# A layer pair of segmented memory attention: the second scores without their wait for the first half's logarithm, and GpSimd's copies of old rows ordered behind the fold

## The chip, the cores and the metric

The kernel runs on one core of a Trainium2 chip. The metric is the device time of one launch in microseconds (us). The core has five engines that run side by side and wait for each other through semaphores: TensorE (PE in the profile; its weight loads are PEld), VectorE (DVE), ScalarE (ACT), GpSimd (POOL) and SyncE (SP, which here only issues DMAs). Each engine works through its instructions in order.

## The reference

Two layers of the same form, each an attention with a recurrent memory (A) and then a gated MLP (B). The attention runs through 64 segments of 32 rows. Eight rows of memory stand in front of each segment, and the first eight rows of the output are the memory of the next segment, so segment after segment must wait for the one before.

```
for s in range(n_seg):                      # 2048 / 32 = 64
    h = concat([mem, xs])                   # 8 + 32 rows of 512
    q, k, v = h @ Wq, h @ Wk, h @ Wv        # 32 heads of 128
    p = softmax(where(mask, q k^T * scale, -1e9))
    o = (p @ v) @ Wo
    mem = o[:8]; outs.append(o[8:])
x = x + A(layernorm(x)); x = x + B(layernorm(x))   # twice
```

## The kernel before

**Tiling.** A block is 128 rows, four segments; j4 is a segment's place in its block and tb the block. Queries and keys of a segment's 24 new rows and 8 memory rows are made in the segment itself, from hT. The last eight rows of every segment are "old rows": their queries, keys and values are known without the memory and are made a block ahead by `b_units`, in pieces that `fill()` puts between the segment's own products. Their source is hB, a GpSimd copy (L637, called by `ln_turn` in a segment with j4 = 0) of the normalized rows that a DMA transpose brought into hT. Their results land by DMA transposes in the tiles KTB and QTB (in the profile: "front" or "old").

**A set of copies.** `prep_segment(s)` moves a segment's old rows from there into QQ (L877, one copy) and KX (L881, one copy for each half r of the heads), on GpSimd. QQ and KX have two buffers (NKQ = 2), so segments s and s + 2 share one. `prep_segment(s + 1)` stands at the end of segment s in the code.

**A segment in order** (`segment`, L905 and on). The products of queries and keys (L714) go through ScalarE (L924) and VectorE (transposes, L927) into QQ and KA. `scores(0)` (L950 for the new keys, L954 for the old keys in KX) writes the first bank of psS; `exps(0)` (L959) and `close(0)` (L962, the exponentials times the mask, giving E) follow. `sums_zero` (L976) adds up the weights of the first half into psS[:, 0, 224:384], called pN. `inverse` makes their reciprocal in RN, as a logarithm (L1017) and an exponential (L1018) on ScalarE. `scores(1)` writes the second bank of psS. Because both halves are in one tile, the scheduler would let it wait for every reader of the tile; `other_bank` declares some of these readers no dependency. Then come `exps(1)`, `close(1)` (the second L962), the division of the first half's weights by their sums (`divide_main` L992, `divide_own` L997), the sums of the second half (`sums_one`, L987), the products with the values (L1004, L1007) and the output product (L790, L797). The fold (L887, L889 and `build_hA` with L896 and L897) adds the parts of that product up, writes the memory of the next segment to memT in two halves of 64 columns (k = 0, 1) and transposes them into hT.

**Order.** PE, DVE and ACT are in the order in which the code is written. The instructions of GpSimd and SyncE are put in order by the scheduler, from its own estimate of when each is ready; what stands ahead in that order is waited for. GpSimd also issues DMAs: loads and stores of the rows that the residual is added to (L222, L224, L229, L240), and near the end of a layer the loads of the MLP's weights (L173, L174). In the last four segments of a layer it adds rows itself (L228), behind a small copy that orders it (`seen`, L1179).

Of the kernel before, what the change touches and what calls it, by code (L numbers as in the profile page):

```python
# [9 lines left out]
ACT = mybir.ActivationFunctionType  # L10
# [4 lines left out]
P = 128  # L15
# [654 lines left out]
def a_block(tc, c, rows, front, MV_in, RS_in, MV_out, RS_out, ahead, wo, S, first):  # L670
    nc = tc.nc
# [5 lines left out]
    with ExitStack() as ctx:  # L677
# [39 lines left out]
        def other_bank(mms, *reads):  # L717

            for m in mms:
                for r in reads:  # L720
                    tc.declare_no_dep(m.ins, r.ins, reason="another bank of the tile")

        memT = [pers.tile([P, P], BF16, name=f"memT{i}") for i in range(2)]
        NKQ = 2
        KAr = [pers.tile([P, 2, 8, 32, 2], BF16, name=f"KA{i}") for i in range(2)]
        QQr = [pers.tile([P, 2, 8, 40, 2], BF16, name=f"QQ{i}") for i in range(NKQ)]
        KXr = [pers.tile([P, 4, 2, 32], BF16, name=f"KX{i}") for i in range(NKQ)]
# [145 lines left out]
        def prep_segment(s, eng=nc.gpsimd):  # L873
            tb, j4 = s // 4, s % 4
            bs = blk_state[tb]
            QQ = QQr[s % NKQ]
            eng.tensor_copy(QQ[:].rearrange("p r n q two -> p (r n) two q")[:, :, :, 32:40],  # L877
                            bs["QTB"].rearrange("p r (n two) k -> p (r n) two k", two=2)[:, :, :, 8 * j4:8 * j4 + 8])
            KX = KXr[s % NKQ]
            for r in range(2):  # L880
                eng.tensor_copy(KX[:, :, r].rearrange("p g (k i) -> p i g k", i=4),  # L881
                                      bs["KTB"][:, r].rearrange("p (i g) k -> p i g k", i=4)[:, :, :, 8 * j4:8 * j4 + 8])
            seg_state[s] = dict(QQ=QQ, KX=KX, VX=bs["VX"])

# [20 lines left out]
        def segment(s, fill, spare1, spare2, spare3, tail, loads):  # L905
            tb, j4 = s // 4, s % 4
            st = seg_state.pop(s)
            QQ, KX, VX = st["QQ"], st["KX"], st["VX"]
            KA = KAr[s % 2]
# [9 lines left out]
            def qk_mm(j, ps, kts=range(KT)):  # L919
                return mm_chunk(ps, lambda kt, cg: hA_cur[:, kt, :], lambda kt, cg: qk_rhs(w, j, kt, cg), kts)  # L920
# [5 lines left out]
            def qk_T(j, r):  # L926
                nc.vector.transpose(out=(QQ[:, j % 2, :, 0:32] if j < 2 else KA[:, j % 2]).bitcast(F32).rearrange("p n q one -> p n (q one)"), in_=r[:].bitcast(F32))  # L927

            def v_mm(r, ps, kts=range(KT)):
                return mm_chunk(ps, lambda kt, cg: hA_cur[:, kt, :], lambda kt, cg: cols_rhs(w, 4 + r, kt, cg), kts)  # L930

            def ends(q):

                return q.rearrange("p h (b e) -> p h b e", e=8)[:, :, 0:5:4, :]

            def own(q):

                return q.rearrange("p (i b e) -> p i b e", i=4, b=2)
# [4 lines left out]
            def scores(r):  # L943

                pS = psS[:, r, :]
                mms = []
                for i in range(4):
                    for g in range(4):
                        n = 4 * i + g
                        mms.append(nc.tensor.matmul(pS[32 * g:32 * g + 32, 40 * i:40 * i + 40], lhsT=KA[:, r, n // 2, :, n % 2], rhs=QQ[:, r, n // 2, :, n % 2],  # L950
                                                    start=(i == 0), stop=True, tile_position=(0, 32 * g), skip_group_check=True))
                for g in range(4):
                    q = QQ[:, r].rearrange("p (i g) q two -> p i g two q", i=4)[:, :, g // 2, g % 2, :]
                    mms.append(nc.tensor.matmul(own(pS[32 * g:32 * g + 32, 160:224]), lhsT=KX[:, g, r, :], rhs=ends(q),  # L954
                                                start=False, stop=True, tile_position=(0, 32 * g), skip_group_check=True))
                return mms

            def exps(r):
                return nc.scalar.activation(out=S[:, r], in_=psS[:, r, 0:224], func=ACT.Exp, scale=scale)  # L959
# [53 lines left out]
            def hview(t, r, lo, hi):  # L1013
                return t.rearrange("p (r g n) q -> p r g n q", r=2, g=2)[:, r, :, :, lo:hi]

            def inverse(out, src):
                nc.scalar.activation(out=out, in_=src, func=ACT.Ln)  # L1017
                return lambda: nc.scalar.activation(out=out, in_=out, func=ACT.Exp, scale=-1.0)  # L1018

            def rview(R, q):  # L1020
                return R[:].rearrange("p g (n q) -> p g n q", q=q)
# [16 lines left out]
            qk_mm(3, psK[:, 0, :], (0, 1, 2))  # L1038
            psS = att.tile([P, 2, 512], F32, name="psS")
            scores(0)  # L1040
            exp0 = exps(0)
            qk_mm(3, psK[:, 0, :], (3,))
            r3, read = qk_rows(psK[:, 0, :])
            if begin:
# [3 lines left out]
            pN = psS[:, 0, 224:384]  # L1048
            sums_zero(pN)
            RN = segp.tile([P, 160], F32, name="RN", bufs=1)  # L1050
            invert = inverse(RN[:], pN)
            invert()
            qk_T(3, r3)
            nc.vector.tensor_copy(VA[:, 0].rearrange("p i e -> p (i e)"), psK[:, 1, :])
            if j4 == 0 and tb + 1 < NB and not begin:
# [2 lines left out]
                fill()  # L1058
            psW = accB.tile([P, 512], F32, name="psV")
            v_mm(1, psW, (0, 1))  # L1060
            other_bank(scores(1), exp0)
            v_mm(1, psW, (2, 3))
            exps(1)
            nc.scalar.copy(VA[:, 1].rearrange("p i e -> p (i e)"), psW[:])
# [14 lines left out]
            if not begin:  # L1079
                fill()  # L1080
            pT = psT[:, :, 0:320].rearrange("p g (n q) -> p g n q", q=40)
            inverse(rview(Rm, 8), pT[:, :, :, 0:8])()
            nc.vector.tensor_tensor(out=uM[1], in0=oview(1, 0, 8), in1=rview(Rm, 8), op=ALU.mult)
            Rt = segp.tile([P, 2, 256], F32, name="Rt", tag="Rt", bufs=1)
            invert = inverse(rview(Rt, 32), pT[:, :, :, 8:40])
            nc.scalar.copy(uT_[0], oview(0, 8, 32))
            nc.scalar.copy(oL[0], oview(0, 32, 40))
# [31 lines left out]
            if s + 1 < NSEG:  # L1119
                prep_segment(s + 1)  # L1120
# [14 lines left out]
        start = nc.vector if first else nc.gpsimd  # L1135
        rows.begin(start)
        prep_segment(0, start)
        due, ys = [], []
        seen = pers.tile([P, 1], BF16, name="seen")
# [16 lines left out]
        for s in range(NSEG):  # L1156
# [78 lines left out]
            def loads():  # L1235
                if due and s < NSEG - 1 and (not ys or tb == NB - 1):
# [7 lines left out]
                    else:  # L1244
                        y_load(y, wo.VX[0][:].rearrange("p j r e -> p (j r e)").bitcast(F32))

            segment(s, lambda n=1: [next(more, None) for _ in range(n)], spare1, spare2, spare3, tail, loads)
        assert due == [NB - 5] and ys == [[NB - 6, True]]
        for k in range(3):
# [57 lines left out]
```

## Time and profile before

| | us |
|---|---|
| median of 3 runs (lowest, highest) | 1660.8 (1657.8, 1661.63) |
| the profiled execution | 1662.02 |
| its span, first to last instruction | 1660.3 |
| granted TensorE clock | 0.997 |
| one segment: first scores to the next segment's first scores, median | 10.3 |
| GpSimd, L881 KX<-old, 128 copies | 63.8, mean 0.522 each |
| GpSimd, L877 QQ<-old, 64 copies | 40.3, mean 0.630 each |
| VectorE, L962 E<-S,maskN, 256 products | 119.0, mean 0.465 each |
| GpSimd, L637 hB<-hT, 30 copies: idle before them, until the DMA hT<-ln_xn | 159.2 |

In lines of the timeline the columns are the start in us from the beginning of the span, the length in us, the engine, the source line, the operation, output<-inputs, the sizes (partitions x elements) and the count; a bracket gives the engine's idle time before and what ended it. In the groups of a page the columns are busy time and mean length of one in ns, then the idle time before. A matmul's end is modelled, and GpSimd's spans are rough.

### The profile page before, as it was taken

What the parts mean: (1) busy time and instruction counts of PE and PEld (TensorE: products, weight loads), DVE (VectorE), ACT (ScalarE), POOL (GpSimd) and SP (SyncE); (2) the same over time, 40 slices, a digit from 0 to 9 for tenths busy, and PEclk for the clock granted to TensorE, in tenths of its full rate; (3) what the DMA queues carried; (4) which work ended last, traced back from release to release, by engine and by line L of the source; (5) the groups of instructions that cost most, each with busy time, mean ns of one, the idle gap of its engine ahead of it and who ended that gap; (6) DMA issues with size and microseconds to landing.
All of it is one profiled execution on the core that took longest, in us unless ns stands there. A gap on an engine that the chain in (4) does not pass through costs nothing.

```text
span 1660.3 us, 88316 instructions
## 1 busy us (share of the span) xinstructions
PE 1603.2 (97%) x39646; PEld 981.6 (59%) x39646; DVE 1117.0 (67%) x3308; ACT 1038.0 (63%) x2409; POOL 306.2 (18%) x604
## 2 busy tenths in 40 slices
PE   5799999999999999999999999999999999999999
PEld 2455566666666666566655556666666666665565
DVE  3566667767777777785466666666677667767722
ACT  2577777777777777661047777777777777766400
POOL 5111111112211222320011111111122112214100
PEclk9999999999999999999999999999999999999999
DMA  9211111112321333277961111112233223335697
GB/s 364 80 42 42 42 41 42 42 42 74 80 55 42 73 84 83 90 171 153 201 179 45 46 47 43 47 42 47 60 91 78 51 55 96 87 68 157 145 202 159
DMA packets 263603, 148.85 MB, mean 90 GB/s; under 512 B 197560, under 2 KB 239648, under 8 KB 263224
## 3 DMA queue, kind: packets, MB, share of 16 engines
q1 hardware_dynamic: 249992, 99.38, 26.9%
q0 software_dynamic: 13232, 43.82, 8.2%
q8 instruction: 310, 5.08, 1.3%
q14 instruction: 69, 0.57, 0.1%
HBM read 59.68 MB, written 37.19 MB: 58 GB/s over the span
## 4 chain that ended last, share of the span: by engine, by line
PE 88%; DVE 5%; DMA 3%; ACT 1%; issue 1%; POOL 0%; SPq 0%; DVEq 0%; POOLq 0%; ACTq 0%
PE psK L714 13%; PE psQ L714 12%; PE psb L714 10%; PE pg L397 9%; PE px L790 7%; PE psO L797 7%; PE psm L714 7%; PE psV L714 6%; PE pwB L809 3%; PE psS L950 3%; PE pz L296 3%; PE psT L987 3%; PE py L440 2%; PE psO L1004 2%; DMA Wk_sb<-in_A_Wk_dram 1%; PE psO L1007 1%
## 5 line engine op out<-in xcount | busy, mean ns | idle before, releaser
L714 PEld LDWEIGHTS <-hT 128*32 128x32 bf16 x12288 | 323.7, 96 | 249.6 <-DVE hT L897 44.9
L924 ACT CAST rows<-psQ 128x512 bf16<-128x512 f32 x256 | 147.9, 588 | 115.1 <-PE psQ L714 114.9
L927 DVE STREAM_TRANSPOSE QQ<-rows 128x256 f32<-128x256 f32 x256 | 113.8, 444 | 120.9 <-ACT rows L924 120.4
L714 PE MATMUL psV<-Wv_sb,hT 128*32 128x512 bf16 x2048 | 157.7, 378 | 0.0
L397 PE MATMUL pg<-z,wspT 128*128 128x344 bf16 x1024 | 154.5, 309 | 0.2 <-DMA wspT<-in_B_w_sp_dram 0.2
L714 PE MATMUL psK<-Wk_sb,hT 128*32 128x512 bf16 x2048 | 152.4, 379 | 0.0
L714 PE MATMUL psQ<-Wq_sb,hT 128*32 128x512 bf16 x2048 | 136.8, 381 | 12.7 <-DVE hT L897 7.5
L927 DVE STREAM_TRANSPOSE KA<-rows 128x256 f32<-128x256 f32 x256 | 113.9, 445 | 51.0 <-ACT rows L924 39.3
L797 PE MATMUL psO<-Wo_high,uT 128*32 128x128 bf16 x8192 | 137.6, 219 | 0.5 <-issue 0.5
L714 PE MATMUL psm<-Wq_sb,hT 128*32 128x512 bf16 x2048 | 136.0, 381 | 1.3
L790 PE MATMUL px<-Wo,uT 128*32 128x256 bf16 x3840 | 134.5, 274 | 1.8 <-DVE uT L1077 1.8
L714 PE MATMUL psQ<-Wk_sb,hT 128*32 128x512 bf16 x2048 | 136.2, 381 | 0.0
L714 PE MATMUL psK<-Wv_sb,hT 128*32 128x512 bf16 x2048 | 134.2, 378 | 0.0
L962 DVE TENSOR_TENSOR E<-S,maskN 128x448 bf16<-128x448 bf16 x256 | 119.0, 465 | 19.1 <-ACT S L959 2.3
L397 PEld LDWEIGHTS <-wspT 128*128 128x128 bf16 x1024 | 100.1, 98 | 53.7 <-DMA wspT<-in_B_w_sp_dram 0.5
L797 PEld LDWEIGHTS <-uT 128*32 128x32 bf16 x8192 | 127.3, 97 | 2.4 <-issue 0.6
L714 PEld LDWEIGHTS <-hB 128*32 128x32 bf16 x2976 | 85.6, 97 | 72.2 <-issue 19.2
L950 PEld LDWEIGHTS <-KA 128*32 128x32 bf16 x4096 | 67.6, 94 | 83.9 <-DVE KA L927 51.0
L959 ACT ACTIVATE S<-psS 128x224 bf16<-128x224 f32 x256 | 91.8, 359 | 38.8 <-PE psS L954 30.2
L881 POOL COPY KX<-old 128x128 bf16<-128x128 bf16 x128 | 63.8, 522 | 267.6 <-PE psS L954 122.9
L790 PEld LDWEIGHTS <-uT 128*32 128x32 bf16 x4096 | 97.8, 96 | 23.4 <-DVE uT L1077 20.3
L881 POOL COPY KX<-front 128x128 bf16<-128x128 bf16 x126 | 62.2, 521 | 248.2 <-PE psS L954 101.5
(205 smaller groups left out, 3019.1 us busy)
## 6 DMA issues: line engine op xcount, KB each, us to landing
o_d<-o_sb SPq DMA_DIRECT2D x126, 64.0 KB
vb_d<-front SPq DMA_DIRECT2D x30, 256.0 KB
VX<-vb_d SPq DMA_DIRECT2D x120, 64.0 KB
ln_x<-xd SPq DMA_DIRECT2D x26, 256.0 KB
y_o<-o_d POOLq DMA_DIRECT2D x22, 256.0 KB, 3.5
xd<-y_o POOLq DMA_DIRECT2D x22, 256.0 KB, 3.1
Wq_sb<-in_A_Wq_dram POOLq DMA_DIRECT2D x8, 512.0 KB, 8.4
Wk_sb<-in_A_Wk_dram POOLq DMA_DIRECT2D x8, 512.0 KB, 10.0
```

Source lines behind the costliest of these rows:

```text
L296: nc.tensor.matmul(pz[:, c0:c1], lhsT=xnT[:, kt, :], rhs=w_in_sb[:, kt, c0:c1], start=(kt == 0), stop=(kt == KT - 1))
L397: nc.tensor.matmul(pg[t][:, k, 0:344], lhsT=wsp[t][:, st, :], rhs=z(st, 344 * k, 344 * k + 344), start=(st == 0), stop=(st == NT - 1))
L714: return [nc.tensor.matmul(ps[32 * cg:32 * cg + 32, :], lhsT=lhs(kt, cg), rhs=rhs(kt, cg), start=(kt == 0), stop=(kt == KT - 1), tile_posi ...
L790: nc.tensor.matmul(px[at:at + 32, 0:256], lhsT=lhs[:, h, :], rhs=wo_rhs(h, slice(k + 2, None, -2) if h % 2 else slice(k, None, 2)), start= ...
L797: nc.tensor.matmul(pw[32 * cg:32 * cg + 32, :], lhsT=lhs[:, h, :], rhs=wo_rhs(h, cg), start=False, stop=(h == H - 1), tile_position=(0, 32 ...
L809: nc.tensor.matmul(pwB[32 * t:32 * t + 32, :], lhsT=src[:, h, :], rhs=wo.head(h).rearrange("p (kt g el) -> p g kt el", kt=4, g=4), start=( ...
L881: eng.tensor_copy(KX[:, :, r].rearrange("p g (k i) -> p i g k", i=4), bs["KTB"][:, r].rearrange("p (i g) k -> p i g k", i=4)[:, :, :, 8 * ...
L924: return r, nc.scalar.copy(r[:].rearrange("p (n el two) -> p n el two", n=8, two=2), ps.rearrange("p (n two el) -> p n el two", n=8, two=2))
L927: nc.vector.transpose(out=(QQ[:, j % 2, :, 0:32] if j < 2 else KA[:, j % 2]).bitcast(F32).rearrange("p n q one -> p n (q one)"), in_=r[:]. ...
L950: mms.append(nc.tensor.matmul(pS[32 * g:32 * g + 32, 40 * i:40 * i + 40], lhsT=KA[:, r, n // 2, :, n % 2], rhs=QQ[:, r, n // 2, :, n % 2], ...
L959: return nc.scalar.activation(out=S[:, r], in_=psS[:, r, 0:224], func=ACT.Exp, scale=scale)
L962: nc.vector.tensor_tensor(out=E[:, r], in0=S[:, r].unsqueeze(1).to_broadcast([P, 2, 224]), in1=maskN[:], op=ALU.mult)
```

## The change

There are two parts. In `segment`, the logarithm on pN is put in the list of readers that `other_bank` declares to be no dependency of `scores(1)`: it reads the first bank, the scores write the second. In `prep_segment`, for every segment but the first, a one-column copy of memT[s % 2] goes into a place of QQ ahead of the QQ copy, and one into a place of KX ahead of each KX copy. The copies that follow overwrite these places, so no value changes. The column is the last of memT, which the second half of the fold writes.

```diff
@@ prep_segment
             QQ = QQr[s % NKQ]
+            if s > 0:
+                eng.tensor_copy(QQ[:, 0, 0, 32:33, 0], memT[s % 2][:, P - 1:P])
             eng.tensor_copy(QQ[:].rearrange("p r n q two -> p (r n) two q")[:, :, :, 32:40],
                             bs["QTB"].rearrange("p r (n two) k -> p (r n) two k", two=2)[:, :, :, 8 * j4:8 * j4 + 8])
             KX = KXr[s % NKQ]
             for r in range(2):
+                if s > 0:
+                    eng.tensor_copy(KX[:, 0, r, 0:1], memT[s % 2][:, P - 1:P])
                 eng.tensor_copy(KX[:, :, r].rearrange("p g (k i) -> p i g k", i=4),
                                       bs["KTB"][:, r].rearrange("p (i g) k -> p i g k", i=4)[:, :, :, 8 * j4:8 * j4 + 8])
@@ segment
-            def inverse(out, src):
-                nc.scalar.activation(out=out, in_=src, func=ACT.Ln)
+            def inverse(out, src, log=None):
+                (log if log is not None else []).append(nc.scalar.activation(out=out, in_=src, func=ACT.Ln))
                 return lambda: nc.scalar.activation(out=out, in_=out, func=ACT.Exp, scale=-1.0)
...
             scores(0)
-            exp0 = exps(0)
+            reads = [exps(0)]
...
-            invert = inverse(RN[:], pN)
-            invert()
+            inverse(RN[:], pN, reads)()
...
-            other_bank(scores(1), exp0)
+            other_bank(scores(1), *reads)
```

## The prediction

> **What bounds the kernel now.** I read the page first: the shares of the engines and the chain that ended last.
>
> ```profile
> PE 1603.2 (97%) x39646; PEld 981.6 (59%) x39646; DVE 1117.0 (67%) x3308; ACT 1038.0 (63%) x2409; POOL 306.2 (18%) x604
> PE 88%; DVE 5%; DMA 3%; ACT 1%; issue 1%; POOL 0%; SPq 0%; DVEq 0%; POOLq 0%; ACTq 0%
> ```
>
> TensorE ends the chain nearly everywhere, so a saving counts only where TensorE stands still. A mean over the span can't show that, so next I read the timeline of one segment (number 45 of 128, start and length in us).
>
> ```profile
> 515.55 0.45 DVE L927 STREAM_TRANSPOSE KA<-rows 128x256 f32<-128x256 f32 x1
> 515.62 0.62 PE L714 MATMUL psV<-Wv_sb,hT 128*32 128x512 bf16 x8
> 515.91 0.30 ACT L1017 ACTIVATE RN<-psS 128x160 f32<-128x160 f32 x1 [0.39 <-PE psS L976]
> 516.05 0.38 PEld L950 LDWEIGHTS <-KA 128*32 128x32 bf16 x16 [0.31 <-DVE KA L927]
> 516.24 0.34 ACT L1018 ACTIVATE RN<-RN 128x160 f32<-128x160 f32 x1
> 516.26 0.28 PE L950 MATMUL psS<-QQ,KA 128*32 128x40 bf16 x16
> 516.65 0.36 ACT L959 ACTIVATE S<-psS 128x224 bf16<-128x224 f32 x1
> 516.74 0.70 POOL L877 COPY QQ<-old 128x256 bf16<-128x256 bf16 x1 [1.49 <-PE psS L954]
> 516.83 0.83 PE L714 MATMUL psb<-Wq_sb,hB 128*32 128x512 bf16 x12
> 517.04 0.59 DVE L962 TENSOR_TENSOR E<-S,maskN 128x448 bf16<-128x448 bf16 x1
> 517.68 0.37 PE L987 MATMUL psT<-E,ones 64*128 64x320 bf16 x4
> ```
>
> Two stops are here. The weights of the second scores (KA, done at 516.00) load at 516.05, but the first product starts at 516.26, 0.05 us after the logarithm of L1017 ends at 516.21; in all 128 segments that distance is 0.05. And L962 takes 0.59 us while GpSimd copies QQ; the sums at L987 start 0.05 after it ends. Next the same stretch of segment 46, where GpSimd copies no QQ at that moment:
>
> ```profile
> 527.45 0.83 PE L714 MATMUL psb<-Wq_sb,hB 128*32 128x512 bf16 x12
> 527.66 0.39 DVE L962 TENSOR_TENSOR E<-S,maskN 128x448 bf16<-128x448 bf16 x1
> 528.21 0.36 PE L987 MATMUL psT<-E,ones 64*128 64x320 bf16 x4
> ```
>
> L962 takes 0.39 and ends at 528.05; L987 starts 0.16 later, behind the products of the fill. Counted over the trace, the second L962 of a segment takes over 0.5 us in 85 segments of 128. From the first scores to the first product of L790 these take 4.38 us in the median (j4 = 0: 4.45), the other 43 take 4.26.
>
> **Part one, the logarithm.** One wait goes in each segment. What ends last then? KA allows a load at 516.05; the eight value products before it start at 515.62 and leave two rounds of 0.21 us (the spacing of four 512-column products in the trace), so TensorE is free at 516.05 too. The scores can start at 516.06 to 516.16 (at once, or after a load of 0.10), that is 0.10 to 0.20 earlier; I take 0.14, between the ends because a load is partly covered by the wait today. Nothing else has to move: the exponential of L1018 stays, and L959 behind it on ScalarE is ready by then. In the 43 free segments TensorE leads into L987, so 43 x 0.14 = 6.0 us (4.3 to 8.6). In the other 85 alone this part would give nothing much, since L962 decides there.
>
> **Part two, the copies leave the closing products.** A set of old-row copies (one QQ, two KX) runs a segment and more ahead today, in the middle of a segment. Now three one-column copies of memT go in front of each set, 378 in all, and the set overwrites that column. In the built program's order the first waits for the second L896 of the fold (k = 1); QQ and KX follow. GpSimd starts 0.16 to 0.18 us after what releases it (L881 behind L954); there VectorE runs L897, L902, L1115 and L927. In today's trace these take the same under a GpSimd copy as without: 246 and 245 ns, 252 and 251, 541 and 540, 445 and 445. So the place is free for VectorE and the second L962 falls to 0.39 everywhere.
>
> With both parts, L987 starts at the later of two: TensorE's products (a free segment's 3.31 us after the first scores, less 0.14) or L962. L962 starts when S is there (0.03 behind L959) and L992 has gone on; between L992 and L962 lie 0.37 at least and 0.42 mostly in the trace, so it gains 0 to 0.06, ends at 3.09 to 3.15 and allows L987 at 3.14 to 3.20. TensorE's 3.17 lies between. Against today's 3.40 in contended segments that is 0.20 to 0.26, and from L987 on the free segments are faster by a further 0.03 (L1007 waits for L997 today). I take 0.255 (0.23 to 0.29): 85 x 0.255 = 21.7 us (19.5 to 24.7). Gain of both parts: 27.7 us (23.8 to 33.3).
>
> At L992 a rule differs from the row. The Trainium skill, GPSIMD Engine Reference, section 8 (Key points), says that GpSimd contends with VectorE instructions that have two SBUF inputs. L992 has two, yet its median is 492 ns with a copy beside it and without; were it stretched like the others and fell to its shortest, 450 ns, the gain would be up to 85 x 0.04 = 3.6 us larger. I keep the row.
>
> **Part three, what the copies now wait for, and what waits behind them.** GpSimd works in order. A set costs, from the first small copy: 0.20 for a 128x1 copy (L1179), 0.30 from the end of a GpSimd instruction to one that waits for it (the store behind L228), then QQ, then KX 0.38 later, and 0.47 for KX:
>
> ```profile
> 37.55 0.47 POOL L877 COPY QQ<-front 128x256 bf16<-128x256 bf16 x1
> 37.94 0.72 POOL L881 COPY KX<-front 128x128 bf16<-128x128 bf16 x2
> ```
>
> That is 0.20 + 0.30 + 0.38 + 0.47 = 1.35 us to the first KX, plus 0.1 to 0.2 to start and some 0.15 until TensorE sees it (from 0.05, what VectorE needs, to 0.30): 1.65 us. Normally there is time: from the fold to the first scores lie 3.2 to 3.3 us. But in the built order the hB copy (L637), which waits for a DMA transpose of the next block's rows, stands ahead of the set in the first segment of a block; today it stands behind sets that are long done. In segment 116 a weight load (L173) stands between as well:
>
> ```profile
> 1395.17 0.29 POOL L637 COPY hB<-hT 128x128 bf16<-128x128 bf16 x1 [4.71 <-DMA hT<-ln_xn]
> 1395.69 0.54 POOL L173 DMA_DIRECT2D front<-in_B_w_in_dram  x1 [0.23 <-issue]
> ```
>
> The first scores there start at 1396.04 today, so their KX would come 1.7 us late. Taking the margin from hB's end (or that load's) to the first KX product for all 28 such segments, 13 have less than 1.65 us; the shortfalls sum to 8.7 us. With 1.30 us for a set they sum to 4.3, with 2.20 to 17.9.
>
> In the last segment of each layer the set stands behind the row additions, and behind two weight loads:
>
> ```profile
> 1513.23 0.54 POOL L173 DMA_DIRECT2D front<-in_B_w_in_dram  x1
> 1513.76 0.54 POOL L174 DMA_DIRECT2D front<-in_B_w_in_dram  x1
> ```
>
> Its KX products are due at 1512.82: 1514.30 + 1.65 - 1512.82 = 3.1 us late; in the first layer 702.04 + 1.65 - 702.64 = 1.05. With the 0.2 that segment 62 gains, 4.6 us (3.9 to 5.7). The DMAs queued behind a set (y loads and stores of 0.54 us issue) are late by the set, about 1.2 us; the trace shows GpSimd idle before most of them. SP's transposes into the old rows wait for reads that end a segment earlier: nothing. The small copies themselves lie on GpSimd, busy 18%.
>
> **Sum.** -27.7 + 8.7 + 4.6 = -14.4 us on the profiled execution's 1662.0 (span 1660.3, 1.7 around it). The median of the runs is 1660.8, 1.2 below that execution; from it, about 1647. The ends: -33.3 + 4.3 + 3.9 gives 1636, -23.8 + 17.9 + 5.7 gives 1661.
>
> **The rivals.**
>
> The copies are never late: the transposes land early enough or a set takes under 1 us. For it: the margins reach 3.0 us. Against: eleven of them are below 1.25, and the last segments' loads are late whatever. With 1.0 us for a set the shortfalls sum to 1.7 and the ends to 3.3: -27.7 + 5, 1638. Chance 0.14.
>
> The stretch of L962 moves instead of going: L962 stays near 0.59 for another reason, or the sums are held by L992 and ScalarE. Then part one gives its 128 x 0.05 (the least that L959 can use), 6 us, against 13 of part three: 1668, slower. Against: the second L962 under a QQ copy take 0.59 us in the median, the others 0.39. Chance 0.05.
>
> Late copies outweigh all. Place: the first scores of a block's first segment and of the last segment, L950 and L954. If each GpSimd copy waits out the one before (0.30 each) and its wake-up is slow, a set takes 3.0 us; then the 28 margins fall short by 36.9 us and the ends by 7.3, so +16.5 us: 1677, slower. It decides from a set of 2.4 us (22.2 + 5.9 us, the gain). For it: extra waits for DMAs stand ahead of QQ and KX in just these segments. Against: two KX copies in a row start 0.27 apart in the trace, so copies overlap. Chance 0.10.
>
> Gain and late copies cancel, a set of 2.2 us with the low gain (-23.8 + 17.9 + 5.7): 1661. Chance 0.08.
>
> **How the numbers follow.** The forecast has 0.63. A measurement can tell about 0.2%, 3.3 us. Faster: 0.63 and 0.14, with 0.02 of the cancelling case, 0.79; within 0.2%: its other 0.06; slower: 0.10 and 0.05. The range, 1635 to 1660, holds the forecast, the never-late case and half of the cancelling one, and leaves out the two slower ones.
>
> **What would show it.** In the changed profile: L950 of the second scores starts within 0.16 us of KA, not 0.05 after L1017; the second L962 is 0.39 in nearly all segments; QQ and KX copies of 0.47 lie within 2 us of the fold; first scores to L790 about 4.12 us. TensorE idles before L950 or L954, released by GpSimd, in some 13 first segments and in the last of each layer, 13 us together. It is wrong if those waits are in most segments, if the copies lie under L962 still, or if L987 stays where it was because L962 starts later.

## The result, and the profile after

The changed kernel takes 1644.9 us in the median of four runs (1641.5 to 1648.0), beside 1660.6 us for the kernel before on the same chip (1657.8 to 1661.6): ratio 0.9908, 95% interval 0.9879 to 0.9937, 0.9% faster. A second set of runs gave 0.9903 (0.9888 to 0.9919). The profiled execution took 1647.84 us with a span of 1646.1, 14.2 us below that of before, at a granted clock of 0.993 (before: 0.997).

The page of the changed kernel, the busy times and the chain that ended last:

```profile
PE 1586.1 (96%) x39646; PEld 967.9 (59%) x39646; DVE 1090.9 (66%) x3308; ACT 1022.8 (62%) x2409; POOL 303.7 (18%) x982
PE 89%; DVE 3%; issue 3%; DMA 2%; ACT 1%; POOL 1%; POOLq 0%; DVEq 0%; ACTq 0%
```

GpSimd has 378 more instructions (982 for 604), yet is busy 2.5 us less: its copies no longer lie beside VectorE's closing products, and are shorter for it (QQ: 0.48 us in the median, 0.70 before). DVE's share of the chain fell from 5% to 3%, and GpSimd, which had none, has 1%. Next the timeline of segment 45, the stretch shown of before (lines 927, 950, 1017, 992, 962 and 987 are now 931, 954, 1021, 996, 966 and 991):

```profile
509.25 0.45 DVE L931 STREAM_TRANSPOSE KA<-rows 128x256 f32<-128x256 f32 x1
509.60 0.31 ACT L1021 ACTIVATE RN<-psS 128x160 f32<-128x160 f32 x1 [0.39 <-PE psS L980]
509.75 0.28 PE L954 MATMUL psS<-QQ,KA 128*32 128x40 bf16 x16
510.31 0.49 DVE L996 TENSOR_TENSOR E<-E,RN 128x320 bf16<-128x320 bf16 x1
510.72 0.38 DVE L966 TENSOR_TENSOR E<-S,maskN 128x448 bf16<-128x448 bf16 x1
511.16 0.37 PE L991 MATMUL psT<-E,ones 64*128 64x320 bf16 x4
```

The second scores start at 509.75, 0.05 us after KA is done (509.70) and while the logarithm still runs (to 509.91). In the median of all segments they start 0.158 before the logarithm's end, where before they started 0.051 after it. The second L966 takes 0.38 instead of 0.59; products over 0.5 us fell from 85 segments to 2. In these two (62 and 127) no copy lies beside L966 but a row addition of GpSimd's (L228), here in segment 62:

```profile
687.03 0.49 DVE L996 TENSOR_TENSOR E<-E,RN 128x320 bf16<-128x320 bf16 x1
687.05 1.48 POOL L228 TENSOR_TENSOR rowsB<-rowsB,y_x 128x512 f32<-128x512 f32 x1 [2.61 <-DMA rowsB<-o_d]
687.44 1.35 DVE L966 TENSOR_TENSOR E<-S,maskN 128x448 bf16<-128x448 bf16 x1
```

The sums at L991 start 3.20 us after the first scores (before: 3.40 in contended segments), and L790 starts 4.15 after them instead of 4.38. The copies now stand right behind the fold, here ahead of segment 25:

```profile
299.39 0.18 DVE L900 TENSOR_TENSOR memT<-psO,t 128x64 bf16<-128x64 f32 x1
...
299.70 0.19 POOL L878 COPY QQ<-memT 128x1 bf16<-128x1 bf16 x1 [6.91 <-DVE memT L900]
299.83 0.30 POOL L884 COPY KX<-memT 128x1 bf16<-128x1 bf16 x2
300.07 0.47 POOL L879 COPY QQ<-front 128x256 bf16<-128x256 bf16 x1
300.46 0.76 POOL L885 COPY KX<-front 128x128 bf16<-128x128 bf16 x2
```

The small copy starts 0.13 us after the fold's second half ends, and QQ takes its undisturbed 0.47. The first KX copy ends 1.24 us after the start of the first small copy (median of all sets), the second 1.54.

Where the 14.2 us come from: summed over the 128 segments, the time from the first scores to L790 fell from 570.8 to 547.9 us, late KX copies included. From L790 to the next first scores (without the step from layer to layer) it rose from 757.6 to 767.0 us; 3.7 of that is the last segment of the second layer, 1.2 segments 52 and 116 (GpSimd's queue, below), and about 2 are two stops of 1 us in which TensorE waits for nothing that the profile shows. The other 2.5 us lie scattered, in both directions, and are not explained. The two stretches together give 13.5 of the 14.2 us.

### The profile page after: what moved, and what is told of

The parts are those of the page before. It is cut to its first block, busy times and chain, and to the rows that moved or that the text cites. A ratio compares the mean times of both kernels' runs of the same rounds, so it can differ in the third digit from the quotient of the medians.

```text
span 1646.1 us, 88740 instructions
## 1 busy us (share of the span) xinstructions
PE 1586.1 (96%) x39646; PEld 967.9 (59%) x39646; DVE 1090.9 (66%) x3308; ACT 1022.8 (62%) x2409; POOL 303.7 (18%) x982
## 4 chain that ended last, share of the span: by engine, by line
PE 89%; DVE 3%; issue 3%; DMA 2%; ACT 1%; POOL 1%; POOLq 0%; DVEq 0%; ACTq 0%
PE psK L714 13%; PE psQ L714 12%; PE psb L714 10%; PE pg L397 9%; PE px L790 7%; PE psO L797 7%; PE psm L714 6%; PE psV L714 6%; PE pz L296 4%; PE pwB L809 3%; PE psT L991 3%; PE py L440 2%; PE psO L1008 2%; PE psS L954 1%; DMA Wk_sb<-in_A_Wk_dram 1%
## 5 line engine op out<-in xcount | busy, mean ns | idle before, releaser
L714 PE MATMUL psV<-Wv_sb,hT 128*32 128x512 bf16 x2048 | 152.4, 380 | 0.0
L878 POOL COPY QQ<-memT 128x1 bf16<-128x1 bf16 x126 | 24.3, 193 | 659.2 <-DVE memT L900 659.2
L790 PE MATMUL px<-Wo,uT 128*32 128x256 bf16 x3840 | 135.3, 275 | 1.9 <-DVE uT L1080 1.9
L714 PEld LDWEIGHTS <-hB 128*32 128x32 bf16 x2976 | 82.2, 96 | 77.6 <-issue 21.7
L966 DVE TENSOR_TENSOR E<-S,maskN 128x448 bf16<-128x448 bf16 x256 | 101.3, 396 | 29.7 <-ACT S L963 28.0
L790 PEld LDWEIGHTS <-uT 128*32 128x32 bf16 x4096 | 98.2, 97 | 23.8 <-DVE uT L1080 19.9
L954 PEld LDWEIGHTS <-KA 128*32 128x32 bf16 x4096 | 57.1, 95 | 73.9 <-DVE KA L931 49.5
L928 ACT CAST rows<-psm 128x512 bf16<-128x512 f32 x128 | 75.1, 587 | 34.8 <-PE psm L714 34.8
```

What stands on the lines that cost most here:

```text
L714: return [nc.tensor.matmul(ps[32 * cg:32 * cg + 32, :], lhsT=lhs(kt, cg), rhs=rhs(kt, cg), start=(kt == 0), stop=(kt == KT - 1), tile_posi ...
L790: nc.tensor.matmul(px[at:at + 32, 0:256], lhsT=lhs[:, h, :], rhs=wo_rhs(h, slice(k + 2, None, -2) if h % 2 else slice(k, None, 2)), start= ...
L928: return r, nc.scalar.copy(r[:].rearrange("p (n el two) -> p n el two", n=8, two=2), ps.rearrange("p (n two el) -> p n el two", n=8, two=2))
L966: nc.vector.tensor_tensor(out=E[:, r], in0=S[:, r].unsqueeze(1).to_broadcast([P, 2, 224]), in1=maskN[:], op=ALU.mult)
```

## The experiments

All were measured beside the kernel before, in three groups. Its median was 1659.3 us for the first four rows, 1659.7 for the next four and 1657.9 for the last three, so rows of different groups compare by their ratios.

| | edit | us, median | ratio, 95% interval |
|---|---|---|---|
| log_alone | part one only | 1655.8 | 0.9976 (0.9967 to 0.9986) |
| copies_alone | part two only | 1657.4 | 0.9982 (0.9969 to 0.9995) |
| no_sets | no copies of old rows | 1631.6 | 0.9834 (0.9819 to 0.9848) |
| long_sets | four more small copies in a set | 1667.0 | 1.0039 (1.0026 to 1.0052) |
| after_again | the changed kernel | 1644.1 | 0.9903 (0.9888 to 0.9919) |
| hb_behind | hB copy behind the set | 1640.9 | 0.9881 (0.9862 to 0.9900) |
| last_free | last segment's set not ordered | 1639.8 | 0.9879 (0.9859 to 0.9898) |
| both_mended | these two | 1636.4 | 0.9862 (0.9843 to 0.9882) |
| last_place | small copies at the last KX product | 1641.9 | 0.9906 (0.9893 to 0.9920) |
| two_signals | one more signal in the scores | 1643.8 | 0.9919 (0.9905 to 0.9932) |
| all_mended | both_mended with last_place | 1629.5 | 0.9829 (0.9815 to 0.9842) |

**Each part alone.** log_alone is the changed kernel without the small copies, copies_alone keeps the wait for the logarithm:

```diff
@@ log_alone: prep_segment, both places
-            if s > 0:
-                eng.tensor_copy(..., memT[s % 2][:, P - 1:P])
@@ copies_alone: segment
-            other_bank(scores(1), *reads)
+            other_bank(scores(1), reads[0])
```

> Part one alone: the second scores no longer wait for the logarithm, GpSimd's copies run ahead as before. Theory (the two parts need each other): the second scores start 0.18 us earlier in every segment, but in the 85 segments where a QQ copy stretches the second L962 to 0.59 us the sums at L987 still start 0.05 us behind it; only the some 43 others gain 0.11 to 0.14. Some 6 to 9 us faster than before: 1652 to 1655 us. Rival (the parts simply add up, and the logarithm's wait is most of the gain): first scores to L790 0.14 to 0.20 us shorter in all 128 segments, 18 to 25 us: 1636 to 1643.

> Part two alone: the copies ordered behind the fold, the wait for the logarithm put back. Theory: the second L962 takes 0.39 us in nearly every segment, but the second scores start 0.05 us behind the logarithm, so first scores to L790 is 4.26 us in all segments: 85 x 0.12 = 10.5 us gained, against some 9 us of late sets (3.6 in first segments of blocks, 5.3 in the two last segments). 1 to 2 us faster than before, within 0.2%: 1659. Rival (the copies alone bring the gain, the logarithm nothing): as the changed kernel, 1645.

Alone the parts give 0.24% and 0.18%, together 0.9%: they need each other. Why shows in the timeline of log_alone, segment 45 again (lines as before the change):

```profile
514.11 0.28 PE L950 MATMUL psS<-QQ,KA 128*32 128x40 bf16 x16
...
514.61 0.48 POOL L877 COPY QQ<-old 128x256 bf16<-128x256 bf16 x1 [1.29 <-PE psS L954]
514.67 0.70 DVE L992 TENSOR_TENSOR E<-E,RN 128x320 bf16<-128x320 bf16 x1
...
515.29 0.47 DVE L962 TENSOR_TENSOR E<-S,maskN 128x448 bf16<-128x448 bf16 x1
...
515.82 0.37 PE L987 MATMUL psT<-E,ones 64*128 64x320 bf16 x4 [0.31 <-DVE E L962]
```

Before, L992 began ahead of the QQ copy (at 516.74 in the prediction's lines) and wasn't stretched:

```profile
516.61 0.49 DVE L992 TENSOR_TENSOR E<-E,RN 128x320 bf16<-128x320 bf16 x1
```

The earlier second scores release GpSimd's QQ copy earlier too (0.49 us after them, 0.48 before), so it now begins 0.06 us ahead of L992, and L992 takes 0.70 instead of 0.49. L962 starts later by what L992 lost, takes 0.47 beside a KX copy, and ends even later than before: in contended segments L790 comes 4.42 us after the first scores in the median (before 4.38), in free ones 4.12 (before 4.26). Summed over the 85 contended segments the stretch is as long as before (377.4 us, before 376.9); the 43 free ones give 3.7 us. So log_alone came out behind the 1652 to 1655 us that was expected. In copies_alone nothing is stretched, but the scores still wait for the logarithm (0.051 after its end), and L790 stands at 4.28 in the median, contended before or not. Over all segments from the first scores to L790 (570.8 us before) copies_alone gains 10.1 us, of which the late copies, shown below, take most back; log_alone gains 3.2, and both together 22.9. Only with both do TensorE and VectorE arrive early at L987.

**What the copies cost.** no_sets has no small copies and, from the third segment of each layer on, no copies of old rows; long_sets makes each set longer:

```diff
@@ no_sets: the QQ copy and the KX copies, in prep_segment
+            if s < 2:
@@ long_sets: behind the first small copy
+                for _ in range(4):
+                    eng.tensor_copy(QQ[:, 0, 0, 32:33, 0], memT[s % 2][:, P - 1:P])
```

> The changed kernel without GpSimd's copies of old rows (and without the small copies ahead of them) from the third segment of each layer on; these segments use the old rows of the first two. It measures what part three costs in all. Theory: no first scores are late, and the last segment of each layer isn't either: some 9 us faster than the changed kernel, 1636 us; first scores to L790 stays at 4.15 us in every segment, as no copy lies under L962 in either. Rival (the late sets are hidden, or the places beside the fold are disturbed by the copies): 1645 with nothing gained, or over 15 us faster with first scores to L790 or the fold shorter.

> The changed kernel with four more one-column copies ahead of each set, each of which waits for the one before: QQ, now last, ends some 1.05 us later than the first KX did. Theory (a set's length decides how late the first scores are where it starts late): a set takes 2.4 to 2.5 us from the hB copy, the margins of the first segments fall short by some 22 us instead of 3.6, the last segments by 2 more; sets that start right behind the fold still end before the first scores. Some 20 us slower than the changed kernel: 1665. Rival (lateness of a set is hidden by TensorE's other work): 1645 to 1648.

Without copies the kernel is another 0.7% faster, so the change gives back about 12 us of what it gains; 2.8 us of a signal and 8.9 us of late copies, both below, make up this sum. The expectation for no_sets had the late copies alone, 9 us and 4.15 us from the first scores to L790; the kernel shows 4.125 there, because the signal goes with the small copies. In long_sets the QQ copy comes last and ends 2.15 us after the start of the set (0.84 in the changed kernel, where the first KX copy, which the scores wait for too, ends at 1.24). TensorE's waits for it, from the view of the waits (waiter <- releaser: sum, count, longest), first in the changed kernel, then in long_sets:

```profile
PE psS L954 <- POOL QQ L879: 5.8, 4, 4.1
PEld L958 <- POOL KX L885: 1.4, 7, 0.2
```

```profile
PE psS L956 <- POOL QQ L881: 24.4, 19, 5.4
```

What the scores wait for thus comes 0.9 us later, and that turns the gain into a loss of 0.4%: 17 us more of waiting in the profile (24.4 - 7.2) and 22 us by the ratios. The profiled execution of long_sets was the fastest of its twelve (1659.2 us); its span is 11.4 us above that of the changed kernel.

**Where the copies are late.** In the changed kernel's segment 116 the set stands behind hB and a weight load:

```profile
1379.30 0.30 POOL L637 COPY hB<-hT 128x128 bf16<-128x128 bf16 x1 [9.23 <-PE psQ L714]
1379.81 0.54 POOL L173 DMA_DIRECT2D front<-in_B_w_in_dram  x1 [0.22 <-issue]
1380.35 0.20 POOL L878 COPY QQ<-memT 128x1 bf16<-128x1 bf16 x1
...
1381.22 0.28 PE L954 MATMUL psS<-QQ,KA 128*32 128x40 bf16 x16 [0.46 <-POOL QQ L879]
...
1381.60 0.10 PEld L958 LDWEIGHTS <-KX 128*32 128x32 bf16 x4 [0.21 <-POOL KX L885]
```

and in the last segment of the second layer behind the row additions and two weight loads:

```profile
1495.46 0.54 POOL L173 DMA_DIRECT2D front<-in_B_w_in_dram  x1
1495.99 0.54 POOL L174 DMA_DIRECT2D front<-in_B_w_in_dram  x1
1496.53 0.20 POOL L878 COPY QQ<-memT 128x1 bf16<-128x1 bf16 x1
...
1497.40 0.28 PE L954 MATMUL psS<-QQ,KA 128*32 128x40 bf16 x16 [4.12 <-POOL QQ L879]
```

The fold that the first small copy waits for had ended 3.0 and 6.7 us before it; it is the place in GpSimd's queue that holds these sets. Counted from the fold, the first KX product of nine segments besides the last ones is later than in the kernel before, by 0.1 to 0.9 us, 3.6 in all: eight first segments of a block (4, 16, 20, 48, 52, 92, 104, 116), and segment 49, whose set stands behind a load of rows (L224) that waits for a DMA. hb_behind puts a small copy from KX into hB ahead of the hB copy, so that the scheduler must place hB after the set; last_free leaves the small copies out in the last segment; both_mended has both:

```diff
@@ hb_behind: turn(..., behind), ahead of the hB copy (L637)
+        if behind is not None:
+            self.nc.gpsimd.tensor_copy(hB[:, 0, 0:1], behind)
@@ segment
-                ln_turn(tb + 1)
+                ln_turn(tb + 1, behind=KX[:, 0, 1, 0:1])
@@ last_free: prep_segment, both places
-            if s > 0:
+            if 0 < s < NSEG - 1:
```

> The changed kernel with the hB copy ordered behind the set of its segment, by a one-column copy from KX into hB ahead of it. Theory: a set no longer waits for the DMA transpose of the next block's rows, so the first scores of a block's first segment are on time (first scores to the first KX product 0.10 us again everywhere), and hB, needed only at the fill some 2.5 us after the first scores, comes in time: some 3.5 us faster than the changed kernel, 1641. Rival (the lateness is the transposes of KTB and QTB or something else, not hB): unchanged, 1645; or hB itself comes too late for the fill, slower.

> The changed kernel, with the last segment's set of each layer not ordered behind the fold. Theory: it runs a segment or two ahead again, before the row additions and the weight loads on GpSimd, so the last first scores are not late by 1.0 and 4.3 us: some 5 us faster than the changed kernel, 1640, less 0.2 where the copies lie under L962. Rival (the end of a layer is held by the row additions themselves): 1645.

> Both of these together. Theory: they are separate places, so the gains add up: some 8.5 us faster than the changed kernel, 1636.5, close to the kernel without any sets. Rival: under 4 us together.

> The changed kernel itself, timed beside these on the same chip: 1645, 0.9 to 1.0% faster than before. It says how far executions of one kernel lie apart here; late first scores in the same segments as in its first profile (4, 16, 20, 48, 49, 52, 92, 104, 116 and the last two) if hB's margins decide.

All medians came within 1 us of what was expected: 3.3 us from the hB copy, 4.3 from the last segments, 7.7 from both, though executions of one of these kernels lie up to 8 us apart. The traces agree: in hb_behind no first segment of a block waits for GpSimd any more, in last_free the last segments don't, and in both_mended one wait for GpSimd of 0.2 us is left on TensorE's weight loads (segment 49). Only the places missed in after_again: beside the last segments, TensorE waits for GpSimd in 8, 20, 49, 52 and 88 there, in 16, 20, 49, 52 and 116 in the first profile, where the same segments were expected. hB moves them: in segment 8 the set starts right behind hB both times, 2.0 us behind the fold in the first profile and 2.5 in after_again.

**The signal.** One thing was in no forecast: in the changed kernel the first exponential starts 0.426 us after the first scores, before 0.400, and everything behind it is 0.025 later. The scores start their products at the same distances in both. The scores' products of the built programs differ in what they signal: the small copy overwrites a place that the first of the four KX products of a half reads, so this product must signal its end as well as the last one, in 112 segments of 128. In the other 16 of the same execution, without that signal, it is 0.400. It is 0.426 in copies_alone too, and 0.400 in log_alone and no_sets, which have no small copies. Three kernels test it: the small copies go to the place that the last KX product reads, or the QQ one stays and the KX one goes to the second:

```diff
@@ last_place
-                eng.tensor_copy(QQ[:, 0, 0, 32:33, 0], memT[s % 2][:, P - 1:P])
+                eng.tensor_copy(QQ[:, 0, 1, 32:33, 1], memT[s % 2][:, P - 1:P])
...
-                    eng.tensor_copy(KX[:, 0, r, 0:1], memT[s % 2][:, P - 1:P])
+                    eng.tensor_copy(KX[:, 3, r, 0:1], memT[s % 2][:, P - 1:P])
@@ two_signals
-                    eng.tensor_copy(KX[:, 0, r, 0:1], memT[s % 2][:, P - 1:P])
+                    eng.tensor_copy(KX[:, 1, r, 0:1], memT[s % 2][:, P - 1:P])
```

> The changed kernel with the one-column copies put where the last of the four KX products of a half reads (QQ of head 3, KX of group 3) instead of the first. In the changed kernel the first KX product of the first scores also signals another engine (so that GpSimd may overwrite that place) in 112 of the 128 segments; there the first exponential starts 0.426 us after the first scores, and in the 16 segments without that signal 0.400, as before. Theory (the extra signal delays the last one by 0.026 us): with the new place only the last product signals, the exponential starts at 0.400 in all segments, sums_zero, the logarithm and KA follow 0.025 earlier, and 112 x 0.025 = 2.8 us are gained: about 1641.5 us, ratio 0.9887. Rival (the 0.026 us come from the wait of TensorE for GpSimd at the first scores): 0.426 stays and the time is the changed kernel's, 1644 to 1645, ratio 0.990.

> The changed kernel with the KX one-column copies put where the second of the four KX products reads; the QQ one stays at the first. In the first scores of 112 segments the first, the second and the last KX product now signal. Theory (each extra signal delays the last): the first exponential starts about 0.452 us after the first scores in these segments and at 0.400 in the other 16; the time is 112 x 0.025 = 2.8 us more than the changed kernel's, 1647 to 1648, ratio 0.992. Rival (no matter what signals): 0.426 and 1644 to 1645, ratio 0.990.

> The version with the hB copy behind the set and the last segment's set not gated (1636.4 us, ratio 0.9862), with the one-column copies at the place that the last KX product reads. Theory of the extra signal: 108 x 0.025 = 2.7 us less, about 1633.7 us, ratio 0.9844. Rival: unchanged, 1636.4, ratio 0.986.

Segment 45 in the timelines of the changed kernel, of last_place and of two_signals, first scores and first exponential:

```profile
507.96 0.28 PE L954 MATMUL psS<-QQ,KA 128*32 128x40 bf16 x16
...
508.38 0.36 ACT L963 ACTIVATE S<-psS 128x224 bf16<-128x224 f32 x1 [0.25 <-PE psS L958]
```

```profile
505.45 0.28 PE L954 MATMUL psS<-QQ,KA 128*32 128x40 bf16 x16
...
505.85 0.36 ACT L963 ACTIVATE S<-psS 128x224 bf16<-128x224 f32 x1 [0.23 <-PE psS L958]
```

```profile
505.48 0.28 PE L954 MATMUL psS<-QQ,KA 128*32 128x40 bf16 x16
...
505.93 0.36 ACT L963 ACTIVATE S<-psS 128x224 bf16<-128x224 f32 x1 [0.28 <-PE psS L958]
```

ScalarE's idle time before the exponential is 0.23 us with no extra signal, 0.25 with one, 0.28 with two. The medians over the 112 segments are 0.400, 0.426 and 0.452, and L790 follows at 4.125, 4.150 and 4.176; the 16 other segments have 0.400 in all three. The rival, a wait of TensorE for GpSimd's copies, falls away: last_place has as many KX weight loads with such a wait as the changed kernel (253), and 0.400. So the signal is the cause of the 0.026 us. The whole time doesn't resolve 2.8 us here: last_place, at 0.9906, lies with the changed kernel (0.9908 and 0.9903) and not at the 0.9887 that was expected, and two_signals hit its 0.992, but their intervals overlap. Single executions of one kernel differ by more than the effect (1641.5 to 1648.0 for the changed kernel, with granted clocks of 0.996 and 0.993 in the fastest and slowest). all_mended is at 0.9829, below the interval of both_mended (0.9843 to 0.9882), though by twice the 2.7 us that the signal explains; the other half is not explained.

all_mended is the fastest version, 1.7% below the kernel before and as fast as no_sets (0.9834): within what these runs resolve, what the copies cost is gone. Its chain that ended last, and its last segment of the second layer, where the scores now wait for KA alone:

```profile
PE 92%; DVE 4%; ACT 2%; DMA 1%; issue 1%; POOL 0%; DVEq 0%; ACTq 0%; POOLq 0%
```

```profile
1479.87 0.28 PE L956 MATMUL psS<-QQ,KA 128*32 128x40 bf16 x16 [1.34 <-DVE KA L933]
```

## Why the prediction was right, and where its steps were not

The forecast of 1647 us was met within 0.13%, and the changed profile's span fell by 14.2 us where the sum said 14.4. (From the median of the runs that sum gives 1646.4.) The mechanism was right: the wait for the logarithm went, the copies left the closing products, and sets came late in the places that were named. That the number is so close is partly luck: the gain was taken 2.8 us too large and the late copies 4.4 us (13.3 for 8.9), which partly cancel, while single executions of the changed kernel lie up to 6.5 us apart.

**Part one.** The second scores start 0.19 to 0.21 us earlier, not 0.14: they follow KA by 0.054. What reaches L790 in a free segment is nevertheless 0.14 (4.26 to 4.12 in log_alone), but for another reason than the one given: L962 becomes the last to arrive at L987, where the step had TensorE lead. That in the 85 contended segments this part alone "would give nothing much" came true in the sum (377.4 us, before 376.9), again for another reason: L992 is stretched there, since a copy that the scores release moves along with them; 30 first segments of a block have 0.02 less in the median, most of the others 0.04 more. The step had not followed what the moved scores release. (Its distance of 0.05 from the logarithm holds in 127 segments of 128; in the first it is 0.71.)

**The row against the rule at L992.** I kept the row, 492 ns with a copy beside it and without. It was read too coarsely: in all 83 overlaps of before, L992 had started first, by 0.128 us in the median, and there it is the copy that pays (0.70 instead of 0.47, though it also runs under L962, and its loss can't be divided between the two). In 80 overlaps of log_alone the copy started first, by 0.067, and L992 takes 0.699, the copy 0.478. The Trainium skill (GPSIMD Engine Reference, section 8, Key points) has the rule that VectorE instructions with two SBUF inputs contend with GpSimd, and log_alone bears it out. The Trainium skill's page SBUF — State Buffer, section Who interferes with whom, says for two-port modes that the one that issues first holds the shared ports and the other is blocked. The order is as the runs here show it, but L992 as the later one loses 0.21 of some 0.41 us of overlap, not all of it. In the changed kernel neither overlaps, so the forecast did not suffer.

**Part two.** Right in mechanism and place: the second L966 is at 0.39 us in the median and over 0.5 in two segments only, VectorE beside the fold is not slowed, and L991 starts at 3.20, the upper end of the 3.14 to 3.20 given (3.17 in last_place, without the extra signal). "About 4.12" from the first scores to L790 is 4.150; the missing term is the extra signal, 112 x 0.025 = 2.8 us, and without it the kernel shows 4.125.

**Part three.** A set was mis-sized. Right behind the fold the first KX is there, as TensorE sees it, after 0.13 + 1.24 + 0.05 = 1.42 us. Behind hB, where it matters, the step to start falls away, since the first small copy begins 0.06 us before the record of the hB copy ends: 1.23 us and not 1.65. The 0.30 taken for the step from the small copy to QQ came from a DMA issue behind an addition; from copy to copy it is 0.17. With 1.24 the prediction's own margins fall short by 3.6 us, in ten segments, and 3.6 us is what the late segments cost (nine of them) instead of 8.7; hb_behind recovers 3.3. The last segments cost 5.3 us (1.0 in the first layer, 4.3 in the second) instead of 4.6: in the second layer the set was shorter than thought, but its KX products fell due 19.4 us earlier than before and the weight loads ended only 17.8 earlier. They were the one place where a wait of microseconds came, as forecast.

The gain itself can be read where neither the signal nor late copies remain: no_sets is 27.7 us below the kernel before of its group (1631.6 and 1659.3), all_mended 28.5 (1629.5 and 1657.9); the forecast had 27.7. Put together with the measured costs: -27.7 + 2.8 + 3.6 + 5.3 = -16.0 us, against -15.7 by the medians of the runs.

**The rivals.** "Never late" failed in the last segments above all, and is what both_mended makes of it: 1636.4, where that rival had 1638. "The stretch moves" didn't happen in the changed kernel, but it is just what log_alone does, onto L992. "Late copies outweigh" needed a set of 2.4 us; long_sets, with QQ there 2.15 us after its set's start, is past the point where gain and loss cancel, at +0.4%.

## What to carry to other kernels

When an instruction is let go earlier, ask what its end releases on other engines and which instruction that will now start ahead of: here half the change alone shifted a copy by 0.2 us and lost its gain in two thirds of the segments. An order that is enforced on an in-order queue is only as good as what the scheduler puts ahead of it; order the long waiters (here hB, the weight loads) behind the urgent work too, or leave the order out where the queue is long. And a dependency has a price on the side that signals: put it where the instruction that reads is the one that signals last anyway.

## What the hardware showed that was not expected

An extra signal from an earlier TensorE product of a group of four delays the moment at which ScalarE starts on the last one's signal by 26 ns, and two by 52 (0.400, 0.426 and 0.452 us after the first scores). The starts of the products don't show it, and their ends are modelled.

Of two overlapping instructions, L992 on VectorE with two SBUF inputs and the QQ copy on GpSimd, the one that starts later is stretched, by 0.21 to 0.23 us at 0.37 to 0.41 us of overlap, and the earlier by no more than 0.01. A start 0.13 us ahead or 0.07 behind decides which. How much is lost depends on the pair and not on the overlap alone: in log_alone L962 starts 0.30 behind a KX copy, overlaps it by 0.40 and takes 0.47 instead of 0.39. Beside a row addition (L228, f32, two inputs) that started 0.39 ahead of it, the second L966 of segment 62 takes 1.35 instead of 0.38, which is nearly all of the 1.09 us of overlap.

A one-column copy on GpSimd takes 0.19 us, and the next copy that waits for it starts 0.17 us after its end; TensorE sees the end of a GpSimd copy after 0.05 us. Its cost on the engine was small (24 us for 126 of QQ, in the shadow), but in a chain it adds up: four more of them put the QQ copy of long_sets 1.31 us further back from the start of its set.
